# Keys turned in 32x32 blocks by VectorE and placed by GpSimd, in place of TensorE transposes, from the third block on

## Chip, core and metric

The kernel runs on one core of a Trainium2 chip. The metric is the device time of one execution in microseconds (us). TensorE is called PE there (PEld is its loading of weights), VectorE DVE, ScalarE ACT, GpSimd POOL, and SyncE, which issues most of the DMAs, SP.

## What is computed

A gated linear attention over 768 tokens (4 sequences, 8 heads of 48) is followed by a two-layer feed-forward with squared relu (384 to 2048 to 384), all in float32:

```python
f = 1.0 / (1.0 + np.exp(-f_logit))
for t in range(S):
    state = f[:, :, t, :, None] * state + np.einsum('bhd,bhe->bhde', k[:, :, t], v[:, :, t])
    y[:, :, t] = np.einsum('bhd,bhde->bhe', q[:, :, t], state)
x = y.transpose(0, 2, 1, 3).reshape(B * S, H * D)
g = np.maximum(x @ w_in, 0.0) ** 2
out = g @ w_out
```

## The kernel before

**Tiling.** The tokens are cut into six blocks of 128 tokens of each sequence (512 columns). A block of attention consists of four units, numbered through from 0 to 23: three "own" units hold 48 rows of each of two heads and 16 rows of the last two heads; the fourth ("last") unit of a block works on those 16-row pieces, which the own units collect in `last_kq` and `last_kn`. Inside a unit the 128 tokens are two halves of 64 (`c` = 0 and 1); tokens meet within a half by a masked matrix of scores, and the state is carried from half to half. The state's increments (keys times values, `add_one`, L537) need the keys with tokens on partitions, while they arrive with channels on partitions: so a unit's keys are turned (`turn`, four TensorE transposes, L511, into a bank of PSUM) and copied out by ScalarE (`turned`, L517 to `kn`, L519 to `last_kn`).

**Feed-forward.** float32 products are made of three rounded ones (high by low, low by high, high by high). A block has 16 steps (`flow`): nine matmuls into a bank `ph` (`up`, L241); relu, square and a rounded copy `gh` on ScalarE (L251 to L253); the rest `gl` on VectorE (L258); and, two steps later, nine matmuls into the output (`down`, L268). Two banks `ph` take turns, so a step's `up` needs the `gl` of two steps before.

**Order.** Each engine works strictly through its own list; only GpSimd's list is laid out by the scheduler. Blocks 0 and 1 of the attention (units 0 to 7) and the first weights are placed by hand (`FIRST`, `SECOND`). Everything later is hooked into the feed-forward's 90 steps. Unit 8 has its slot at step 12, unit 9 at 15, unit 10 at 18 and so on (`SLOTS`); the matmuls of a unit's scores and increments and of the outputs of the unit before it run at the end of that step (`slot`). `STAGE_AT` says how many steps ahead of its slot each part of an own unit runs: loads (`L`, `v`), gates and decayed keys (`GK`: a scan L449, GpSimd's L454 and the multiplication L455), queries (`Q`: L461, the scan L463, L466), the turn (`TN`), the crossing of states (`s`). A hook at place 0 stands ahead of a step's `up`, at 0.5 between ScalarE's squares and VectorE's `gl`, at 1 behind `down`. `LAST_AT` is for last units. During steps 1 to 14 the second half of the weights is decoded as well (ScalarE L138, VectorE L147, L149, L153, ScalarE's L166, VectorE's L168).

In a slot the increments of the first half (c = 0) come first, those of the second half last; a small GpSimd memset (L746) stands between the two, and the second half waits for it. From unit 8 on the transposes and the increments use one bank, `shared`.

Of the kernel before, what the change touches and what calls it, by code (L numbers as in the profile page):

```python
# [13 lines left out]
F32 = mybir.dt.float32  # L14
# [8 lines left out]
P = 128  # L23
B, H, S, D = 4, 8, 768, 48
DM, DFF = 384, 2048
HP = H // 2
C = 64
TB = 128
NBLK = S // TB
NC = TB // C  # L30
# [3 lines left out]
ROWS = 64 + D  # L34
# [12 lines left out]
NBUF = 3  # L47
# [7 lines left out]


SLOTS = (12, 15, 18, 21, 23, 27, 31, 35, 39, 43, 47, 51, 55, 59, 63, 67, 71)
STAGE_AT = ((-6, 0, "Lv"), (-3, 1, "GK"), (-1, 0.5, "Q"), (-1, 1, "TN"), (1, 1, "s"))
LAST_AT = ((-6, 0, "v"), (1, 1, "s"))


FIRST = """
# [301 lines left out]
def fast_path(ctx, psum, tc, moe, ident, low, flag, fkqT, vN, w, w4, out):  # L364
    nc = tc.nc
    V, G = nc.vector, nc.gpsimd
# [17 lines left out]
    for r in (0, C):  # L384
        G.affine_select(
            out=mask[r : r + C], in_=mask[r : r + C], compare_op=ALU.is_ge, fill=0.0,
# [19 lines left out]
    class Unit:  # L406
# [30 lines left out]
                nc.sync.dma_start(self.fkq[:, c, :NT], fkqT[self.blk, self.hp, :, c])  # L437

        def load_v(self):
            self.vn = self.wk([P, B, 2 * D], "vn", NBUF + 1)  # L440
            nc.sync.dma_start(self.vn, vN[self.blk, self.hp])

        def gates(self):
# [56 lines left out]

        def turn(self):

            if self.blk < 2:
                self.pk = self.ps_a[0].tile([P, B, P], F32, tag="pk", name=f"pk{self.nm}")
            else:

                if not shared:
                    shared.append(self.ps_a[0].tile([P, B, P], F32, tag="pk", name="shared"))
                self.pk = shared[0]
            for b in range(B):  # L510
                nc.tensor.transpose(  # L511
                    out=self.pk[:, b], in_=self.kt[:, b * TB : (b + 1) * TB], identity=ident
                )

        def turned(self):
            self.kn = self.wk([P, B, ROWS], "kn")
            nc.scalar.copy(out=self.kn, in_=self.pk[:, :, :ROWS])  # L517
            at = self.hp * (C - D)
            nc.scalar.copy(  # L519
                out=last_kn.rearrange("p b (h r) -> p b h r", h=2)[:, :, :, at : at + C - D],  # L520
                in_=self.pk.rearrange("p b (h r) -> p b h r", h=2)[:, :, :, D:],
            )

        @cached_property
# [8 lines left out]

        def add_one(self, dd, b, c, h):

            rows, m = slice(c * C, (c + 1) * C), D if h or self.blk > 1 else C
            return nc.tensor.matmul(  # L537
                dd[h * C : h * C + m, c, b * D : (b + 1) * D],
                lhsT=self.kn[rows, b, h * C : h * C + m],
                rhs=self.vn[rows, b, h * D : (h + 1) * D], start=True, stop=True,  # L540
            )
# [116 lines left out]
        def stage(self, letters):  # L658
            for c in letters:
                {  # L660
                    "L": lambda: self.load(slice(0, 3)),
                    "f": lambda: self.load(slice(0, 1)),
                    "k": lambda: self.load(slice(1, 2), slice(2, 3)),
                    "v": lambda: self.load_v(),
                    "G": lambda: self.gates(),
                    "K": lambda: self.keys(),
                    "Q": lambda: self.queries(),
                    "m": lambda: self.move(),
                    "r": lambda: self.crossed(),
                    "T": lambda: self.turn(),  # L670
                    "N": lambda: self.turned(),
                    "D": lambda: self.add(),
                    "S": lambda: self.scores(),
                    "M": lambda: self.masked(),
                    "C": lambda: self.states(),
                    "s": lambda: self.crossed_states(),
                    "Y": lambda: self.outputs(),
                    "H": lambda: self.upper(),
                    "z": lambda: self.less(),
                    "X": lambda: self.lower(),  # L680
                    "g": lambda: self.parts((1,), G if self.blk < 2 else nc.sync),
                    "h": lambda: self.parts((0,), nc.sync),
                }[c]()
# [5 lines left out]
    ps_a = moe.ps_a = psum.enter_context(  # L689
        tc.tile_pool(name="ps_a", bufs=1, space=bass.MemoryType.PSUM)  # L690
    )
    half = list(range(LO)), list(range(LO, NF))
    xs = {blk: moe.new_x(blk, blk) for blk in range(2)}
    units, decoding, shared = {}, {}, []
# [13 lines left out]
    def slot(old, new):  # L708

        ab = ps_a.tile([P, 2, 512], F32, tag="ab", name=f"ab{(new or old).nm}_{new is None}")
        rows = [[], []]
        if old:
            old.py = ab[:, :, : B * C]
            for c in range(NC):
                for b in range(B):
                    for part in range(2):
                        for h in (c, 1 - c):  # L720
                            rows[c].append((C, lambda a=(part, b, c, h): old.output_one(*a)))
        if new:
            new.sd = ab[:, :, B * C :]
            new.dd = shared[0].rearrange("p (c e) n -> p c (e n)", c=NC)[:, :, : B * D]
            adds = [
                [] if new.last_of(c) else [
                    (D, lambda a=(b, c, h): update(*a)) for b in range(B) for h in (c, 1 - c)
                ] for c in range(NC)
            ]
            for h in range(2):  # L730
                for b in range(B):
                    for c in (h, 1 - h):
                        rows[h].append((C, lambda a=(b, c, h): new.score_one(*a)))
            rows = [adds[0] + rows[0], rows[1] + adds[1]]
        seen = []

        def behind(ins, first):
            tc.add_manual_dep(ins, first.name, mybir.DependencyInfo(
                mybir.DependencyClass.Sync, mybir.DependencyReason.DATA
            ), reason="one bank")  # L740

        def update(b, c, h):
            ins = new.add_one(new.dd, b, c, h).ins
            if c == 0 and b == B - 1 and h:

                seen.append(G.memset(tick, 0).ins)  # L746
                behind(seen[0], ins)
            elif c and b == 0 and h:
                behind(ins, seen[0])

        at = [0, 0]
        while any(rows):
            r = min((r for r in range(2) if rows[r]), key=lambda r: at[r])
            cols, do = rows[r].pop(0)
            at[r] += cols
            do()
# [51 lines left out]
    with tc.manual_schedule(engines={ET.PE, ET.SP, ET.DVE, ET.Activation}):  # L808
# [13 lines left out]
        def hook(n, at, do):  # L822
            hooks.setdefault((max(n, 0), at), []).append(do)
# [38 lines left out]
        for at, old, un in zip(SLOTS, (None, *late), (*late, None)):  # L862
            if un:
                for n, place, stage in STAGE_AT if un.own else LAST_AT:
                    hook(at + n, place, lambda un=un, stage=stage: un.stage(stage))
            hook(at, 1, lambda old=old, un=un: slot(old, un))
            if old:
                hook(at, 1, lambda old=old: old.stage("HX" if old.own else "HXhg"))
            if un:
                hook(at, 1, lambda un=un: un.stage("rMCm" if un.own else "rMC"))  # L870
# [155 lines left out]
@with_exitstack  # L1026
def tile_kernel(ctx: ExitStack, tc: tile.TileContext, fkqT, vN, w, w4, out):
    nc = tc.nc
    const = ctx.enter_context(tc.tile_pool(name="const", bufs=1))
    ident = const.tile([P, P], F32, name="ident")  # L1030
    low = const.tile([P, NBLK * NJ, B * NC], F32, name="low")
    sums = const.tile([P, 2 * NF], F32, name="sums")
    flag = const.tile([1, 2], I32, name="flag")
    moe = Moe(ctx, tc, const, sums, out)
    with ExitStack() as fast:
        last, rv = fast_path(fast, ctx, tc, moe, ident, low, flag, fkqT, vN, w, w4, out)

    last.w = moe.w[HELD]  # L1040

    with tc.If(rv > 0):
        with ExitStack() as gen:
            general_path(gen, tc, moe, ident, fkqT, vN, w, out, last)
    moe.w[HELD] = last.w
    last.g[NF - 1] = moe.held
    moe.finish_last(last, lambda e: out[last.blk, e * P : (e + 1) * P])
# [61 lines left out]
```

## Time and profile before

| what | value |
|---|---|
| median of 3 runs | 491.6 us (489.62 to 492.38) |
| the profiled execution's own time | 489.16 us |
| its span, first to last instruction | 487.5 us |
| granted TensorE clock | 0.997 of full speed |
| busy: TensorE, VectorE, ScalarE, GpSimd | 97%, 53%, 58%, 7% |

Times of the profile are counted from the start of the span; 1.7 us of the execution lie around it. Busy time of an engine is the time in which an instruction of it is recorded as running; matmuls overlap, so TensorE's idle time says more than its busy time.

### The profile page before, as it was taken

The numbers are of one execution on the slowest core, as the hardware profiler recorded it, in microseconds if no ns is written. First come the engines' busy times: TensorE is split into PE (matmuls) and PEld (weight loads), VectorE is DVE, ScalarE is ACT, GpSimd is POOL, SyncE is SP. The second block draws the span as 40 slices with busy tenths as digits, with TensorE's granted clock in tenths as the row PEclk, the third lists the DMA queues.
The fourth block names the chain that finished last, engine by engine and source line by source line (L and its number), as shares of the span: only waits on it lengthen the run. The fifth ranks groups of instructions, "written<-read, shape, count | busy, mean of one in ns | idle before, by whom it ended". The sixth has DMA issues, their size and how long they took to land. (4 is left out here: it accounts for less than half of the span.)

```text
span 487.5 us, 11465 instructions
## 1 busy us (share of the span) xinstructions
PE 472.8 (97%) x4795; PEld 388.2 (80%) x4795; DVE 256.5 (53%) x474; ACT 281.7 (58%) x570; POOL 32.1 (7%) x82
## 2 busy tenths in 40 slices
PE   5889999999999999999999999999999999999996
PEld 5677787888788888888888888888888888888884
DVE  7999966989985355643437443346343212221111
ACT  4777757887676555644546645555655444544451
POOL 6222010001100000000000000000000000000000
PEclk9999999999999999999999999999999999999998
DMA  8985235566134004232005222004210002100002
GB/s 284 309 284 143 58 103 197 205 200 224 29 95 143 17 6 119 94 101 74 1 2 125 94 93 82 1 1 117 87 26 2 2 0 34 66 0 3 0 0 71
DMA packets 22636, 42.60 MB, mean 87 GB/s; under 512 B 4512, under 2 KB 8128, under 8 KB 22576
## 3 DMA queue, kind: packets, MB, share of 16 engines
q1 hardware_dynamic: 22128, 40.86, 27.1%
q0 software_dynamic: 448, 0.92, 0.8%
q8 instruction: 39, 0.64, 0.5%
q14 instruction: 21, 0.17, 0.1%
HBM read 31.69 MB, written 4.72 MB: 75 GB/s over the span
## 5 line engine op out<-in xcount | busy, mean ns | idle before, releaser
L241 PE MATMUL ph<-x,w 128*128 128x512 f32 x864 | 216.4, 395 | 1.8 <-DVE gl L258 1.4
L241 PEld LDWEIGHTS ph<-x,w 128*128 128x128 f32 x864 | 159.4, 188 | 36.5 <-DVE w L168 1.1
L268 PE MATMUL po<-gh,w 128*128 128x512 f32 x570 | 175.6, 389 | 0.0
L258 DVE TENSOR_TENSOR gl<-ph,gh 128x512 fp32r<-128x512 f32 x95 | 65.6, 691 | 172.1 <-ACT gh L253 171.8
L251 ACT ACTIVATE ph<-ph 128x512 f32<-128x512 f32 x96 | 55.9, 582 | 119.7 <-PE ph L241 119.5
L268 PEld LDWEIGHTS po<-gh,w 128*128 128x128 f32 x570 | 107.0, 188 | 22.2
L268 PE MATMUL po<-gl,w 128*128 128x512 f32 x285 | 111.1, 390 | 0.0
L268 PEld LDWEIGHTS po<-gl,w 128*128 128x128 f32 x285 | 53.5, 188 | 11.2
L252 ACT ACTIVATE ph<-ph 128x512 f32<-128x512 f32 x96 | 55.9, 582 | 3.0
L253 ACT CAST gh<-ph 128x512 fp32r<-128x512 f32 x95 | 55.8, 587 | 3.0
L449 DVE TENSOR_TENSOR_SCAN fkq<-fz,dr 128x520 f32<-128x520 f32 x18 | 22.3, 1236 | 6.3 <-ACT fz L444 6.3
L166 ACT CAST w<-wa 128x384 fp32r<-128x384 f32 (+1 forms) x33 | 16.6, 511 | 15.3 <-DVE wa L153 12.3
L454 POOL TENSOR_SCALAR fkq<-fkq 128x8 f32<-128x8 f32 x18 | 13.2, 735 | 145.1 <-DVE fkq L449 136.6
L463 DVE TENSOR_TENSOR_SCAN fkq<-fz,dz 128x520 f32<-128x520 f32 x18 | 22.3, 1242 | 0.6
L602 PE MATMUL ab_False<-sc,vn 64*48 64x64 f32 (+1 forms) x480 | 20.7, 220 | 0.0
L138 ACT ACTIVATE wa<-raw 128x384 f32<-128x384 f32 (+1 forms) x33 | 18.1, 548 | 4.3 <-DMA raw<-in_w_dram 4.2
L631 ACT CAST x<-ab_False 112x512 fp32r<-112x512 f32 x12 | 7.0, 587 | 22.0 <-PE shared L537 16.0
L611 PE MATMUL ab_False<-rx,sx 48*48 48x64 f32 (+1 forms) x240 | 19.4, 216 | 0.0
L647 DVE TENSOR_TENSOR x<-ab_False,x 112x512 fp32r<-112x512 f32 x12 | 8.3, 692 | 20.2 <-ACT x L631 20.2
L149 DVE SCALAR_TENSOR_TENSOR wa<-raw,wa 128x384 int32<-128x384 int32 (+1 forms) x33 | 17.9, 551 | 0.7
L602 PEld LDWEIGHTS ab_False<-sc,vn 64*48 64x48 f32 (+1 forms) x480 | 18.0, 126 | 0.0
L168 DVE TENSOR_TENSOR w<-wa,w 128x384 fp32r<-128x384 f32 (+1 forms) x33 | 17.9, 545 | 0.0
(138 smaller groups left out, 461.5 us busy)
## 6 DMA issues: line engine op xcount, KB each, us to landing
raw<-in_w_dram SPq DMA_DIRECT2D x32, 384.0 KB, 4.3
fkq<-in_fkqT_dram SPq DMA_DIRECT2D x15, 768.0 KB, 5.8
vn<-in_vN_dram SPq DMA_DIRECT2D x24, 192.0 KB, 4.5
out_dram<-ob SPq DMA_DIRECT2D x14, 256.0 KB, 2.4
fkq<-in_fkqT_dram SPq DMA_DIRECT2D x9, 256.0 KB, 4.6
x<-ys SPq DMA_DIRECT2D x30, 64.0 KB, 2.4
last_kq<-fkq SPq DMA_DIRECT2D x28, 64.5 KB, 2.3
out_dram<-part SPq DMA_DIRECT2D x3, 256.0 KB, 2.4
```

The costliest lines, as they stand in the source:

```text
L138: nc.scalar.activation(a, upper_f, AF.Abs, scale=2.0**-112, **kw)
L149: nc.vector.scalar_tensor_tensor(out=h, in0=upper, scalar=-(1 << 31), in1=h, op0=ALU.bitwise_and, op1=ALU.bitwise_or)
L241: self.nc.tensor.matmul(self.cur.ph[f], lhsT=w[:, i], rhs=x[:, j], start=first and n == 0, stop=last and n == 2)
L251: nc.scalar.activation(ph, ph, AF.Relu)
L252: nc.scalar.activation(ph, ph, AF.Square)
L253: nc.scalar.copy(out=gh, in_=ph)
L258: self.nc.vector.tensor_tensor(out=gl, in0=self.cur.ph.pop(f), in1=gh.bitcast(F32), op=ALU.subtract)
L268: self.nc.tensor.matmul(c.po[e], lhsT=l, rhs=r, start=f == c.fs[0] and i == 0, stop=f in c.ends and i == 2, skip_group_check=len(c.ends) > 1,)
L449: V.tensor_tensor_scan(out=rr[:, ::-1], data0=self.fz[:, NZ * CZ : 0 : -1], data1=dr[:, ::-1], initial=0.0, op0=ALU.mult, op1=ALU.add,)
L463: V.tensor_tensor_scan(out=pp, data0=self.fz[:, : NZ * CZ], data1=dz, initial=0.0, op0=ALU.mult, op1=ALU.add)
L602: nc.tensor.matmul(to[:m], lhsT=self.vn[rows, b, h * D : h * D + m], rhs=self.sc[rows, h, b], start=b == 0, stop=none and c == 0 and b == ...
L611: nc.tensor.matmul(to[:m], lhsT=s[rows, b * D : b * D + m], rhs=q[rows], start=False, stop=b == B - 1,)
```

## The change

From unit 8 on the four transposes of an own unit are gone. In their place, for each half `c`, VectorE turns the 32x32 blocks of the half's keys (128 partitions x 256 elements) into a tile `kb` of one buffer, and GpSimd copies the eight 32-partition pieces of it to where they belong in `kn`. The first half is done behind the keys (`GKB`, three steps ahead of the slot), the second behind the queries (`Qb`, one step ahead). ScalarE's copy of the bank into `kn` goes; the copy into `last_kn` stays and reads `kn`. The bank `shared` is now made in `slot` and holds increments alone. Unit 8's increments write 64 rows for one head, as the first to use the bank. The values `vn` are loaded five steps ahead instead of six, into three buffers instead of four.

```diff
-STAGE_AT = ((-6, 0, "Lv"), (-3, 1, "GK"), (-1, 0.5, "Q"), (-1, 1, "TN"), (1, 1, "s"))
-LAST_AT = ((-6, 0, "v"), (1, 1, "s"))
+STAGE_AT = (
+    (-6, 0, "L"), (-5, 0, "v"), (-3, 1, "GKB"), (-1, 0.5, "Qb"), (-1, 1, "N"), (1, 1, "s"),
+)
+LAST_AT = ((-5, 0, "v"), (1, 1, "s"))
+Q = 32
...
-            self.vn = self.wk([P, B, 2 * D], "vn", NBUF + 1)
+            self.vn = self.wk([P, B, 2 * D], "vn", NBUF)
...
+        def turn_blocks(self, c):
+            if c == 0:
+                self.kn = self.wk([P, B, P], "kn")
+            kb = self.wk([P, B, C], "kb", 1)
+            V.transpose(out=kb, in_=self.kt.rearrange("p (b c t) -> p b c t", b=B, c=NC)[:, :, c])
+            for a in range(0, C, Q):
+                for r in range(0, P, Q):
+                    G.tensor_copy(
+                        out=self.kn[c * C + a : c * C + a + Q, :, r : r + Q], in_=kb[r : r + Q, :, a : a + Q]
+                    )
+
         def turned(self):
-            self.kn = self.wk([P, B, ROWS], "kn")
-            nc.scalar.copy(out=self.kn, in_=self.pk[:, :, :ROWS])
+            if self.blk < 2:
+                self.kn = self.wk([P, B, P], "kn")
+                nc.scalar.copy(out=self.kn[:, :, :ROWS], in_=self.pk[:, :, :ROWS])
             at = self.hp * (C - D)
             nc.scalar.copy(
                 out=last_kn.rearrange("p b (h r) -> p b h r", h=2)[:, :, :, at : at + C - D],
-                in_=self.pk.rearrange("p b (h r) -> p b h r", h=2)[:, :, :, D:],
+                in_=(self.pk if self.blk < 2 else self.kn).rearrange("p b (h r) -> p b h r", h=2)[:, :, :, D:],
             )
...
-            rows, m = slice(c * C, (c + 1) * C), D if h or self.blk > 1 else C
+            rows, m = slice(c * C, (c + 1) * C), D if h or self.n > 2 * HP else C
...
+            if not shared:
+                shared.append(ps_a.tile([P, B, P], F32, tag="pk", name="shared"))
             new.dd = shared[0].rearrange("p (c e) n -> p c (e n)", c=NC)[:, :, : B * D]
```

The lists of the engines show it at unit 8. A tile's last number only tells tiles of one name apart, and the changed kernel's lines are numbered 3 to 13 higher from the edit on. VectorE's list around unit 8's queries (`fkq_0_1462` holds its keys and queries, `wa` and `w` are weights being decoded), before:

```order
L461 RECIPROCAL dz<-fkq_0_1462 128x8 [waits Pool_49]
L463 SCALAR_TENSOR_TENSOR fkq_0_1462<-fz_71,dz 128x520 [waits DVE_49]
L466 TENSOR_TENSOR fkq_0_1462<-fkq_0_1462 128x512 [waits DVE_49]
L258 TENSOR_TENSOR gl_11_1689<-ph_11_1678,gh_11_1688 128x512 [waits PE_49,Activation_49]
L168 TENSOR_TENSOR w_1_1697<-wa_1_1673,w_1_1697 128x384 [waits Activation_49]
L147 TENSOR_SCALAR wa_0_1717<-wa_0_1717 128x384 [waits Activation_49]
```

and in the changed kernel:

```order
L464 RECIPROCAL dz<-fkq_0_1462 128x8 [waits Pool_49]
L466 SCALAR_TENSOR_TENSOR fkq_0_1462<-fz_71,dz 128x520 [waits DVE_49]
L469 TENSOR_TENSOR fkq_0_1462<-fkq_0_1462 128x512 [waits DVE_49]
L518 STREAM_TRANSPOSE kb_0_1707<-fkq_0_1462 128x256 [waits Pool_49]
L261 TENSOR_TENSOR gl_11_1700<-ph_11_1689,gh_11_1699 128x512 [waits PE_49,Activation_49]
L171 TENSOR_TENSOR w_1_1718<-wa_1_1684,w_1_1718 128x384 [waits Activation_49]
L150 TENSOR_SCALAR wa_0_1731<-wa_0_1731 128x384 [waits Activation_49]
```

The transpose of the second half stands between the queries and `gl`, and waits for GpSimd (the one buffer of `kb`). ScalarE's list in the same place, before:

```order
L166 CAST w_1_1697<-wa_1_1673 128x384 [waits DVE_49]
L517 COPY kn_0_1714<-shared 128x448 [waits PE_49]
L519 COPY last_kn<-shared 128x8x16
L138 ACTIVATE wa_0_1717,sums<-raw_0_1565 128x384 [waits DMAHW3_49]
L138 ACTIVATE wa_1_1722,sums<-raw_1_1568 128x384 [waits DMAHW4_49]
L166 CAST w_0_1727<-wa_0_1717 128x384 [waits DVE_49,Activation_49]
```

and in the changed kernel:

```order
L169 CAST w_1_1718<-wa_1_1684 128x384 [waits DVE_49]
L530 COPY last_kn<-kn_0_1627 128x8x16 [waits Pool_49]
L141 ACTIVATE wa_0_1731,sums<-raw_0_1565 128x384 [waits DMAHW3_49]
L141 ACTIVATE wa_1_1736,sums<-raw_1_1568 128x384 [waits DMAHW4_49]
L169 CAST w_0_1741<-wa_0_1731 128x384 [waits DVE_49,Activation_49]
```

One copy of the two is left; it now waits for GpSimd, with the next weights' decoding behind it in the list.

## Rows read from the trace of the kernel before

**Rows 1.** The page of the kernel before: busy us, share of the span, instructions.
```profile
PE 472.8 (97%) x4795; PEld 388.2 (80%) x4795; DVE 256.5 (53%) x474; ACT 281.7 (58%) x570; POOL 32.1 (7%) x82
```

**Rows 2.** The windows: busy us per engine, with instructions; granted clock, DMA share, GB/s.
```profile
110.00:150.00 40.00, 39.21 (x354) 31.86 (x354) 35.80 (x66) 28.90 (x65) 4.16 (x8) 1.00 0.34 107
150.00:190.00 40.00, 40.00 (x536) 33.15 (x535) 20.27 (x35) 22.24 (x43) 2.20 (x7) 1.00 0.28 79
```

**Rows 3.** The timeline around one later unit: start us, us, engine, line.
```profile
187.63 0.23 POOL L454 TENSOR_SCALAR low<-fkq 128x8 f32<-128x8 f32 x1
...
188.97 1.24 DVE L463 TENSOR_TENSOR_SCAN fkq<-fz,dz 128x520 f32<-128x520 f32 x1
...
190.25 0.69 DVE L466 TENSOR_TENSOR fkq<-fkq 128x512 f32<-128x512 f32 x1
...
192.21 0.60 PE L511 MATMUL shared<-ident,fkq 128*128 128x128 f32 x4
192.57 2.32 PE L241 MATMUL ph<-x,w 128*128 128x512 f32 x9
...
198.28 0.20 PE L537 MATMUL shared<-vn,kn 64*48 64x48 f32 x1
```

**Rows 4.** The instructions of L511: ns min/median/max, first and last start us.
```profile
L511 PE MATMUL shared<-ident,fkq x48: 270/272/273, 117.8 to 362.0; 128*128 128x128 f32 x48
```

**Rows 5.** Groups by line and shape: busy us, mean ns | idle before.
```profile
L582 DVE TENSOR_TENSOR sp<-state,fkq 112x192 f32<-112x192 f32 x30 | 10.6, 353 | 0.5
...
L149 DVE SCALAR_TENSOR_TENSOR wa<-raw,wa 112x256 int32<-112x256 int32 x1 | 0.4, 424 | 0.0
```

**Rows 6.** The timeline of GpSimd (POOL) at the start.
```profile
1.03 0.19 POOL L395 MEMSET sp<- 112x32 f32 x2
1.25 0.28 POOL masks.py:199 TENSOR_SCALAR_AFFINE_SELECT ident<-ident 128x128 f32<-128x128 f32 x1
1.50 0.53 POOL L385 TENSOR_SCALAR_AFFINE_SELECT mask<-mask 64x64 f32<-64x64 f32 x2
```

**Rows 7.** The timeline at 144.6 us: one of VectorE, one of GpSimd.
```profile
144.58 0.69 DVE L455 TENSOR_TENSOR fkq<-fkq 128x512 f32<-128x512 f32 x1
144.63 0.74 POOL L454 TENSOR_SCALAR fkq<-fkq 128x8 f32<-128x8 f32 x1 [5.99 <-DVE fkq L449]
```

**Rows 8.** The timeline of units 8 and 9; in brackets idle us, releaser.
```profile
119.94 0.27 ACT L519 COPY last_kn<-shared 128x128 f32<-128x128 f32 x1
...
120.10 0.56 ACT L138 ACTIVATE wa<-raw 128x384 f32<-128x384 f32 x1
...
121.10 0.68 DVE L258 TENSOR_TENSOR gl<-ph,gh 128x512 fp32r<-128x512 f32 x1
...
122.16 0.35 DVE L147 TENSOR_SCALAR wa<-wa 128x384 int32<-128x384 int32 x1
...
122.40 0.24 PE L537 MATMUL shared<-vn,kn 64*48 64x48 f32 x1
...
123.22 0.25 PE L537 MATMUL shared<-vn,kn 64*48 64x48 f32 x2
...
123.79 0.52 ACT L166 CAST w<-wa 128x384 fp32r<-128x384 f32 x1 [2.51 <-DVE wa L153]
...
126.06 0.69 DVE L258 TENSOR_TENSOR gl<-ph,gh 128x512 fp32r<-128x512 f32 x1 [0.42 <-ACT gh L253]
...
132.57 0.68 DVE L258 TENSOR_TENSOR gl<-ph,gh 128x512 fp32r<-128x512 f32 x1
...
133.40 2.52 PE L241 MATMUL ph<-x,w 128*128 128x512 f32 x9 [0.77 <-DVE gl L258]
...
138.23 0.68 DVE L258 TENSOR_TENSOR gl<-ph,gh 128x512 fp32r<-128x512 f32 x1
...
139.31 0.20 PE L537 MATMUL shared<-vn,kn 64*48 64x48 f32 x1
```

**Rows 9.** The DMA issues of the page: KB each, median us to landing.
```profile
vn<-in_vN_dram SPq DMA_DIRECT2D x24, 192.0 KB, 4.5
```

More of the change, by code (lines that the diff above doesn't have):

```diff
@@ L501, in turn @@
         def turn(self):
[L503 to L509, printed above, removed]
+            self.pk = self.ps_a[0].tile([P, B, P], F32, tag="pk", name=f"pk{self.nm}")
             for b in range(B):
@@ L670, in stage @@
                     "T": lambda: self.turn(),
+                    "B": lambda: self.turn_blocks(0),
+                    "b": lambda: self.turn_blocks(1),
                     "N": lambda: self.turned(),
```

## Prediction

> **What bounds the kernel now.** I read the busy table first: TensorE works 97% of the span, everything else 58% or less [rows 1]. The windows say where that is not quite true. From 150 us on TensorE is busy in 40.00 of 40.00 us, with VectorE and ScalarE at about half; between 110 and 150 us it is 39.21, and there VectorE is at 35.80 and ScalarE at 28.90, because the second half of the weights is still being decoded [rows 2]. So after 150 us a microsecond taken off TensorE is a microsecond off the time, and anything else is free until its lateness reaches TensorE. Before 150 us VectorE has almost no slack, and the one wait of the stretch shows whom TensorE waits for: the first matmul of a block at 133.40 stood idle 0.77 us for `gl`, VectorE's subtraction [rows 8]. Two of the twelve changed units, 8 and 9 (slots 12 and 15), lie in that stretch; the other ten come behind it.
>
> **What is removed.** Four transposes a unit. In a quiet place the first starts at 192.21 and the next block's first matmul at 192.57: 0.36 us of TensorE for the four. There are 48 of them, so twelve such gaps [rows 3, 4], 4.3 us. Unit 9's stands just ahead of the 133.40 wait and only fills it, so 11 x 0.36 = 4.0 us count at most. ScalarE loses its copy of the turned keys and keeps the 0.27 us one into `last_kn` [rows 8]; after 150 us it is busy for 22 of 40 us [rows 2], so that is worth nothing there.
>
> **What is added on VectorE.** Two transposes of 128x256 a unit. No row has one. The nearest are 353 ns for 112x192 and 424 ns for 112x256 [rows 5]; I take 0.40 us. After 150 us VectorE's idle half hides it.
>
> **What is added on GpSimd.** Sixteen copies a unit of 32 partitions x 128 elements. The only single-input instructions of GpSimd with so many elements are the selects: 0.28 us for 128x128, and two of 64x64 in 0.53 [rows 6]. An instruction of 8 elements lasts 0.23 [rows 3], so most of the price is fixed. I take 0.28 us a copy, 2.24 us for eight. From below: two small memsets took 0.19 us together [rows 6], so if copies on different partitions overlap, 0.10. From above: an 8-element instruction took 0.74 us beside VectorE's two-input multiplication of 0.69, three times its 0.23 [rows 3, 7]; so 0.74 where VectorE is in the way each time. The value is nearest to the select, which reads and writes like a copy.
>
> **Does it fit, behind 150 us?** Take the unit of [rows 3]. GpSimd's two small instructions end at 187.86, and the first eight copies can start at 187.9, behind the first VectorE transpose. The second transpose can't start before L466 ends at 190.94, nor before those eight have read the single `kb`. The keys of the second half are used by the matmul that was at 198.28, now 197.9. So 10.0 us hold sixteen copies, a 0.40 us transpose, and up to 1.9 us in which the scan (1.24) and L466 (0.69) keep GpSimd out: they fit while a copy takes under (10.0 - 0.4 - 1.9) / 16 = 0.48 us. At 0.28 there are 3 us to spare, and all ten units gain: 10 x 0.36 = 3.6 us. ScalarE's `last_kn` copy now stands behind the sixteenth copy, at about 194.5, and holds up the relu of the product begun at 192.57 by little; ScalarE's idle 18 of 40 us take that up [rows 2].
>
> **Units 8 and 9.** Here the new work is late by the length of a busy queue, and two engines queue behind it. The second transpose of unit 8 stands behind L466, which ended where `gl` started, 121.10 [rows 8]; the first one has already pushed that to 121.5. So it ends at 121.9, and the eight copies at 124.15, or 124.65 if one weight subtraction (L168, two inputs) keeps GpSimd out for 0.5 us, as 0.74 against 0.23 in [rows 3, 7].
> - TensorE: the slot begins at 122.40 - 0.36 = 122.04 and uses the second half 0.82 us later (123.22 against 122.40) [rows 8]. It waits from 122.9 to 124.2-124.7.
> - ScalarE: the `last_kn` copy sits in order ahead of the decode's L138 (120.10 before). Now it ends 0.27 us behind the copies, L138 0.56 behind that, so VectorE's L147 moves from 122.16 to 125.0-125.5, 2.9 to 3.3 us. From L147 on the chain had no slack: ScalarE waited 2.51 us for L153, VectorE 0.42 for `gh` [rows 8]. So `gl` of 126.06 moves by as much; from there to the `gl` of 132.57 VectorE ran without a wait, and unit 9's first transpose adds 0.40. That is the very `gl` for which TensorE waited: it restarts not at 133.40 but 3.2 to 3.7 us later. This one number contains the slot's wait and unit 8's saved 0.36.
> - Unit 9: L466 ended where `gl` started, 138.23 [rows 8]; plus 3.3-3.7, plus 0.40, plus eight copies (2.24, or 2.74 beside another L168): 144.1-145.1. The slot's second half was due at 139.31 [rows 8], now at 142.5-143.0: a wait of 1.6 to 2.1 us, with `gl` of the next steps late once more, up to 0.3.
>
> **Sum.** +3.2 to 3.7, +1.6 to 2.1, +0.3, -3.6: between +1.5 and +2.5 us. With contention shown for GpSimd in the rows I take the upper end, +2.5 us: 491.7 us against the profiled execution's 489.2. That execution lies 2.4 us under the median of the runs shown (491.6), so on their scale 494.1. Bounds: at 0.10 us a copy unit 8's chain slips only 1.7 us and unit 9 waits 0.2 and 0.3, sum -1.4; at 0.20 each burst of eight is 0.64 shorter, +0.2 to +1.2; at 0.33 it is 0.4 longer, +2.3 to +3.3; at 0.74 see below. 0.5% is 2.45 us, about what a measurement of this kernel can tell from no change, so the forecast stands on that edge.
>
> The `v` load, with three buffers instead of four and one step later, lands 4.5 us after its issue [rows 9] and is issued five steps ahead, some 20 us (one step and most of a slot lie between 192.57 and 198.28 in [rows 3]). It costs nothing unless it is held for over three steps; unit 12's must now wait for the slot at step 18, one step. Were that cover gone, a unit's slot would wait for what is left of 4.5 us.
>
> **Rivals.**
> 1. *Copies overlap* (0.10 to 0.2 us): sum -1.4 to +1.2, 490.2 to 492.8. For it: the memsets at 0.10 us each [rows 6]. Against: the selects there stand one behind the other, 0.25 us from start to start.
> 2. *Faster*: the whole 11 x 0.36 = 4.0 us and no new wait, 487.6. It needs unit 8's copies to end by 122.9 and the decode's L138 not to matter, which is to say a transpose and eight copies within 1.4 us of L466, and slack in VectorE that [rows 2] don't show. The point of decision: whether TensorE restarts at 133.4 or later.
> 3. *VectorE is held by the copies*. The rows show GpSimd waiting for VectorE (0.74 for 0.23) while the multiplication beside it lasted 0.69 us like the one of [rows 3] beside which GpSimd did nothing; but there GpSimd came second [rows 7]. If a copy that comes first holds a two-input instruction for its own 0.28 us, the eight early copies of unit 8 push VectorE by up to 2.2 us in the stretch without slack: +2.5 + 2.2, 496.3. [...]
> 4. *Copies are slow everywhere* (0.74 us): 16 x 0.74 + 0.4 = 12.2 against 10.0 us, so 2.2 us of waiting in each of ten units, and 3.7 more in each of the two early ones: 494.1 + 22 + 7 = 523. It starts at 0.48 us a copy.
>
> [...]
>
> **How the numbers follow.** Forecast 0.46, copies overlap 0.20, faster 0.13, VectorE held 0.13, slow copies 0.08. The forecast's own range, copies of 0.20 to 0.33 us, is 491.8 to 494.9; its likelier upper part lies about +0.5%, so I give half of it to each side. Faster by over 0.5%: 0.14 (rival 2 and a little of 1). Within 0.5%: the rest of rival 1 and half of the forecast, 0.41. Slower: the other half and rivals 3 and 4, 0.45. For 8 in 10 the range reaches from 488.5 to 501: it leaves out most of rival 2 and all of rival 4.
>
> **What would show it.** No L511 behind 100 us, and TensorE's next matmul 0.36 us sooner at each of ten slots; copies of about 0.28 us in two bursts of eight a unit; TensorE idle for GpSimd in the slots at about 122 and 140 us and nowhere behind 150; the wait for `gl` at about 133 longer by 2 us; ScalarE's `last_kn` copy waiting some 4 us for GpSimd in both units. It is wrong if waits for GpSimd appear in every slot (copies over 0.48 us), if VectorE's instructions get longer beside copies, or if the transposes take much more than 0.4 us.

## The result, and the profile after

| | before | after |
|---|---|---|
| median of 6 runs each, on one chip | 490.88 us (489.62 to 492.38) | 495.96 us (494.3 to 496.91) |
| ratio, 95% interval | | 1.0095 (1.0068 to 1.0123) |
| the profiled execution, its span | 489.16, 487.5 us | 495.62, 493.8 us |

The change makes the kernel 0.95% slower, some 4.7 us by the ratio (5.1 by the medians); +2.5 us was forecast. The busy line of the page of the changed kernel, against [rows 1]:

```profile
PE 471.1 (95%) x4747; PEld 386.3 (78%) x4747; DVE 266.2 (54%) x498; ACT 276.4 (56%) x558; POOL 100.8 (20%) x274
```

TensorE has lost its 48 transposes, and yet it is idle for a larger share. The windows say where: against [rows 2] it is idle for 4.8 us of the stretch from 110 to 150 (0.8 before) and for 2.1 us of the next (nothing before).

```profile
110.00:150.00 40.00, 35.19 (x315) 28.03 (x314) 30.35 (x59) 22.48 (x52) 13.70 (x38) 0.91 0.35 107
150.00:190.00 40.00, 37.94 (x496) 30.98 (x498) 23.02 (x41) 22.09 (x45) 12.76 (x39) 1.00 0.20 63
```

The waits of TensorE, the longest four: line waited for, us in total, times, longest. The changed kernel's lines are numbered up to 15 higher behind the edit (the small memset L746 is L761), and the transposes of units 0 to 7 are L508. The first wait is the increments' second half. The `flag` it names is the small memset between the two halves; here it stands behind the eight copies in GpSimd's list, so a wait for it is a wait for the copies.

```profile
PE shared L548 <- POOL flag L761: 4.5, 3, 2.2
PE ds L548 <- DMA vn<-in_vN_dram: 2.5, 1, 2.5
PE pk L508 <- DVE fkq L458: 2.0, 1, 2.0
PE po L271 <- DVE ob L339: 1.9, 1, 1.9
```

The wait for `pk` stands in every kernel of this study. The one for `vn` is a load at 17 us, long before the change acts: 2.5 us here. It comes and goes with either number of buffers: with four it is 0.5 us in the kernel before and 1.9 in *no turn* (below), with three 0.3 to 0.8 in five kernels (*from unit 10* is one), 1.6 in *copies halved* and 2.2 in *from unit 12*. By step 11 (113.68 before, 115.88 here) the profiled execution is 2.2 us late. I call this lateness the front and count it to no part of the change.

So I follow the lateness of TensorE's steps rather than the sum. The timeline of the changed kernel, TensorE (start us, us), at the first matmuls of the steps:

```profile
119.96 2.23 PE L244 MATMUL ph<-x,w 128*128 128x512 f32 x9
...
127.32 0.34 PE L548 MATMUL shared<-vn,kn 64*48 64x48 f32 x2 [2.25 <-POOL flag L761]
...
139.82 2.63 PE L244 MATMUL ph<-x,w 128*128 128x512 f32 x9 [0.45 <-DVE gl L261]
...
148.22 0.25 PE L548 MATMUL shared<-vn,kn 64*48 64x48 f32 x2 [2.06 <-POOL flag L761]
...
148.72 2.35 PE L244 MATMUL ph<-x,w 128*128 128x512 f32 x9
...
157.04 2.20 PE L244 MATMUL ph<-x,w 128*128 128x512 f32 x9
...
161.81 0.50 PE L271 MATMUL po<-gl,w 128*128 128x512 f32 x1 [1.90 <-DVE ob L339]
...
165.31 2.33 PE L244 MATMUL ph<-x,w 128*128 128x512 f32 x9
...
179.67 0.25 PE L548 MATMUL shared<-vn,last_kn 64*48 64x48 f32 x2 [0.16 <-POOL flag L761]
...
180.18 2.35 PE L244 MATMUL ph<-x,w 128*128 128x512 f32 x9
...
487.40 2.32 PE L271 MATMUL po<-held,w 128*128 128x512 f32 x9 [0.30 <-PEq L1057]
```

The same steps in the timeline of the kernel before, where [rows 8] don't have them:

```profile
118.12 2.31 PE L241 MATMUL ph<-x,w 128*128 128x512 f32 x9
...
139.81 2.33 PE L241 MATMUL ph<-x,w 128*128 128x512 f32 x9
...
148.47 2.33 PE L241 MATMUL ph<-x,w 128*128 128x512 f32 x9
...
154.69 2.33 PE L241 MATMUL ph<-x,w 128*128 128x512 f32 x9
...
169.07 2.33 PE L241 MATMUL ph<-x,w 128*128 128x512 f32 x9
...
480.58 2.33 PE L268 MATMUL po<-held,w 128*128 128x512 f32 x9 [0.30 <-PEq L1042]
```

| up to the start of | before, after | late by | what was added | forecast |
|---|---|---|---|---|
| step 12 | 118.12, 119.96 | 1.84 | front +2.2, unit 8's transposes -0.36 | -0.36 |
| step 15 | 133.40, 139.82 | 6.42 | unit 8, with its -0.36: 6.42 - 2.2 = +4.2 | +3.2 to 3.7 |
| step 16 | 139.81, 148.72 | 8.91 | unit 9: +2.5 | +1.6 to 2.1, and up to 0.3 |
| step 18 | 148.47, 157.04 | 8.57 | unit 10's transposes: -0.34 | -0.36 |
| step 19 | 154.69, 165.31 | 10.62 | the wait for `ob`: +2.05 | none |
| step 22 | 169.07, 180.18 | 11.11 | slot 21: +0.49 | none |
| the last block | 480.58, 487.40 | 6.82 | nine units: -4.29, or -0.48 each | -0.36 each |

Without the front that is 4.2 + 2.5 - 0.34 + 2.05 + 0.49 - 4.29 = +4.6 us.

The `ob` term and the smaller one of slot 21 are those that the prediction didn't have. VectorE and GpSimd at unit 10, in their own timelines:

```profile
156.09 4.02 POOL L521 COPY kn<-kb 32x128 f32<-32x128 f32 x8 [0.29 <-DVE kb L518]
160.65 2.62 POOL L521 COPY kn<-kb 32x128 f32<-32x128 f32 x8 [0.54 <-DVE kb L518]
```

```profile
160.14 0.45 DVE L518 STREAM_TRANSPOSE kb<-fkq 128x256 f32<-128x256 f32 x1 [1.52 <-POOL kn L521]
160.51 0.65 DVE L261 TENSOR_TENSOR gl<-ph,gh 128x512 fp32r<-128x512 f32 x1
161.08 0.68 DVE L339 COPY ob<-po 128x512 f32<-128x512 f32 x1
```

A unit's second transpose waits until GpSimd has read the first half out of the single `kb`, 1.52 us here (1.2 to 1.5 in nine units). Behind it in VectorE's list stand `gl` and, at this step alone of the ten later units, the copy of a finished output bank (`ob`). TensorE's `down` (L271) needs that bank, and it waits 1.90 us.

Slot 21 is that of unit 11, a last unit, and the next own unit's slot, 23, lies only two steps behind it. So unit 12's first eight copies, three steps ahead of its own slot, come ahead of slot 21's memset in GpSimd's list:

```profile
176.89 2.59 POOL L521 COPY kn<-kb 32x128 f32<-32x128 f32 x8 [0.29 <-DVE kb L518]
179.53 0.09 POOL L761 MEMSET flag<- 1x1 int32 x1
```

The bracket in TensorE's list has 0.16 us of idle time, but from the slot's first matmul to its second half it takes 1.89 us (177.78 to 179.67) instead of 1.42 (167.15 to 168.57).

The new pieces by their own lines (times in ns: shortest, median, longest):

```profile
L521 POOL COPY kn<-kb x192: 280/291/1325, 115.5 to 371.8; 32x128 f32<-32x128 f32 x192
L518 DVE STREAM_TRANSPOSE kb<-fkq x24: 439/445/447, 114.9 to 368.9; 128x256 f32<-128x256 f32 x24
```

### The profile page after: what moved, and what is told of

Its sections match the earlier page's. It is cut to its first block, busy times and chain, and to the rows that moved or that the text cites. A ratio compares the mean times of both kernels' runs of the same rounds, so it can differ in the third digit from the quotient of the medians.

```text
span 493.8 us, 11605 instructions
## 1 busy us (share of the span) xinstructions
PE 471.1 (95%) x4747; PEld 386.3 (78%) x4747; DVE 266.2 (54%) x498; ACT 276.4 (56%) x558; POOL 100.8 (20%) x274
## 3 DMA queue, kind: packets, MB, share of 16 engines
HBM read 31.69 MB, written 4.72 MB: 74 GB/s over the span
## 5 line engine op out<-in xcount | busy, mean ns | idle before, releaser
L244 PEld LDWEIGHTS ph<-x,w 128*128 128x128 f32 x864 | 161.4, 189 | 37.5 <-DVE w L171 1.3
L271 PE MATMUL po<-gh,w 128*128 128x512 f32 x570 | 175.9, 390 | 0.0
L271 PEld LDWEIGHTS po<-gh,w 128*128 128x128 f32 x570 | 107.4, 188 | 22.3
L271 PE MATMUL po<-gl,w 128*128 128x512 f32 x285 | 111.6, 392 | 1.9 <-DVE ob L339 1.9
L521 POOL COPY kn<-kb 32x128 f32<-32x128 f32 x192 | 70.2, 366 | 31.0 <-DVE kb L518 21.8
L271 PEld LDWEIGHTS po<-gl,w 128*128 128x128 f32 x285 | 53.8, 189 | 13.6 <-DVE ob L339 2.3
L457 POOL TENSOR_SCALAR fkq<-fkq 128x8 f32<-128x8 f32 x18 | 12.2, 679 | 150.2 <-DVE fkq L452 125.8
L530 ACT COPY last_kn<-kn 128x128 f32<-128x128 f32 x12 | 3.6, 300 | 43.7 <-POOL kn L521 43.7
L466 DVE TENSOR_TENSOR_SCAN fkq<-fz,dz 128x520 f32<-128x520 f32 x18 | 22.4, 1242 | 0.6
L171 DVE TENSOR_TENSOR w<-wa,w 128x384 fp32r<-128x384 f32 (+1 forms) x33 | 18.2, 555 | 0.0
```

The lines of the kernel that those rows point to most:

```text
L171: nc.vector.tensor_tensor(out=w[:, 1], in0=a, in1=w[:, 0].bitcast(F32), op=ALU.subtract)
L244: self.nc.tensor.matmul(self.cur.ph[f], lhsT=w[:, i], rhs=x[:, j], start=first and n == 0, stop=last and n == 2)
L271: self.nc.tensor.matmul(c.po[e], lhsT=l, rhs=r, start=f == c.fs[0] and i == 0, stop=f in c.ends and i == 2, skip_group_check=len(c.ends) > 1,)
L466: V.tensor_tensor_scan(out=pp, data0=self.fz[:, : NZ * CZ], data1=dz, initial=0.0, op0=ALU.mult, op1=ALU.add)
L521: G.tensor_copy(out=self.kn[c * C + a : c * C + a + Q, :, r : r + Q], in_=kb[r : r + Q, :, a : a + Q])
```

## The experiments

The diffs are cut to the parts of lines that differ; `...` stands for lines left out. The experiments ran in two groups of four, each beside 17 runs of the kernel before: medians 490.13 us (488.9 to 491.9) and 489.83 us (489.17 to 492.14). My theory was that units 8 and 9 pay, with the `ob` wait, and the ten later ones gain. The main rivals: every unit pays a little; or the three buffers of values cost something.

### From unit 10

Units 8 and 9 keep TensorE's transposes; three buffers of values stay.

```diff
+EARLY_AT = ((-6, 0, "L"), (-5, 0, "v"), (-3, 1, "GK"), (-1, 0.5, "Q"), (-1, 1, "TN"), (1, 1, "s"))
+FROM = 10
...
-            if self.blk < 2:
+            if self.n < FROM:
...
-                for n, place, stage in STAGE_AT if un.own else LAST_AT:
+                for n, place, stage in (STAGE_AT if un.n >= FROM else EARLY_AT) if un.own else LAST_AT:
```

> Units 8 and 9 keep the TensorE transposes; only units from 10 on use VectorE and GpSimd. Theory A (the loss sits in units 8 and 9, +4.2 and +2.5 us in the profile, and in one wait of 2.05 us at unit 10 for the copy of the output block; every later unit gains 0.42): time of before - 10 x 0.42 + 0 to 2.05, that is 2.1 to 4.2 us under before, 486.7 to 488.8 if before is 490.9; no wait of TensorE for GpSimd at slots 12 and 15. Theory B (every unit pays, by GpSimd and VectorE getting in each other's way): not under before, 491 or more. Theory C (2.2 us of the loss is a wait for the values' DMA at 17 us, made by three buffers): that wait is there too, 2.2 us more than A.

485.94 us (485.2 to 487.63), ratio 0.9931 (0.9911 to 0.995): what was a loss of 0.95% is a gain of 0.7%. What its list of waits still has for GpSimd's `flag` and for the output copy at unit 10:

```profile
PE po L273 <- DVE ob L341: 0.6, 1, 0.6
...
PE shared L555 <- POOL flag L768: 0.2, 1, 0.2
```

The 0.2 us are slot 21's. Followed by its steps, its front aside, it ends 3.3 us ahead of the kernel before. Units 8 and 9 hold the loss; neither the later units nor the three buffers do.

### From unit 12

The same with `FROM = 12`, so that unit 10 keeps TensorE's transposes too.

> Units 8, 9 and 10 keep the TensorE transposes. Theory A: no unit in the stretch of decoding or at the output copy is left, nine gain 0.42: before - 3.8 us, 487.1 if before is 490.9; faster than e1_from10 if unit 10's wait stays there, 0.4 slower if it doesn't. Theory B: not under before. Theory C: 2.2 us more.

486.22 us (485.51 to 487.48), ratio 0.9925 (0.9909 to 0.9942), the same as from unit 10 within the intervals. No wait for `ob` is in its trace, and by its steps without the front it ends 3.9 us ahead of the kernel before, against 3.3 *from unit 10*, where unit 10 loses some 0.5 us on balance. The runs can't tell these two apart.

### Second turn behind `gl`

In all twelve units the second transpose and its copies go behind `gl` and `ob`, to the end of the step.

```diff
-(-1, 0.5, "Qb"), (-1, 1, "N"), (1, 1, "s"),
+(-1, 0.5, "Q"), (-1, 1, "bN"), (1, 1, "s"),
```

> All twelve units changed, but the second transpose stands behind VectorE's gl and the copy of the output block instead of ahead of them. Theory A: the wait at unit 10 (TensorE 1.9 us for the output copy, which stood behind a transpose that waited 1.5 us for the one buffer of its result) goes, units 8 and 9 stay as they are or lose up to 0.6 us more each, since their copies start one gl later: 1 to 2 us under the changed kernel, 494 to 495. If the wait has another cause (GpSimd slowing VectorE itself): no change, 496.

495.08 us (493.8 to 497.0), ratio 1.012 (1.0101 to 1.014): no better than the changed kernel. The `ob` wait is gone, so its cause is the transpose ahead of it. But unit 10's slot now waits for the copies instead (by the steps 0.7 us), and the early units pay more (5.1 and 3.3 us instead of 4.2 and 2.5):

```profile
PE shared L548 <- POOL flag L761: 4.8, 4, 3.0
PE ph L244 <- DVE gl L261: 2.5, 2, 1.9
```

### Late `last_kn`

ScalarE's copy into `last_kn` goes behind the unit's slot, so that the decoding no longer stands behind it.

```diff
-(-1, 0.5, "Qb"), (-1, 1, "N"), (1, 1, "s"),
+(-1, 0.5, "Qb"), (1, 0, "N"), (1, 1, "s"),
```

> All twelve units changed, but ScalarE's copy into last_kn comes two hooks later, at the start of the step after the slot, so nothing of the weights' decoding stands behind it while it waits for GpSimd. Theory A (in unit 8 the delay of the decoding behind that copy costs more than TensorE's own wait for the copies): TensorE's waits in slots 12 and 15 stay at 2.1 to 2.9 us, the gl at step 13 is late no longer, 2.7 us under the changed kernel, 493.3. Rival (only TensorE's direct wait counts): no change, 496.

490.81 us (489.51 to 493.12), ratio 1.002 (1.0005 to 1.0034): most of the loss is gone, more than I expected. The timelines show that this is not the whole story. VectorE decodes on without a gap, so the `gl` that TensorE needs for step 15 (132.57 before, 139.00 in the changed kernel) is at 134.48:

```profile
122.92 0.59 DVE L171 TENSOR_TENSOR w<-wa,w 128x384 fp32r<-128x384 f32 x1
123.44 0.45 DVE L150 TENSOR_SCALAR wa<-wa 128x384 int32<-128x384 int32 x1
...
134.48 0.68 DVE L261 TENSOR_TENSOR gl<-ph,gh 128x512 fp32r<-128x512 f32 x1
```

TensorE waits 3.06 us for the copies, longer than in the changed kernel, because beside VectorE's decoding the eight take 3.71 us (2.85 there), and then goes on at half its clock (granted 0.50 from 128 to 132 us):

```profile
126.39 0.34 PE L548 MATMUL shared<-vn,kn 64*48 64x48 f32 x2 [3.06 <-POOL flag L761]
...
127.41 4.21 PE L244 MATMUL ph<-x,w 128*128 128x512 f32 x9
...
134.19 2.20 PE L244 MATMUL ph<-x,w 128*128 128x512 f32 x9
...
138.27 2.20 PE L244 MATMUL ph<-x,w 128*128 128x512 f32 x9
```

From the end of the wait to the block at 134.19 are 7.80 us; the kernel before takes 127.94 - 123.22 = 4.72 us for the same matmuls. The 3.1 us between are the clock's, and now TensorE waits for nothing at step 15: with the decoding on time, the low clock is the bound there. Step 15 starts 4.9 us later than before, 4.5 without this execution's front of 0.4, which is no better than the 4.2 of the changed kernel. What is saved comes behind it: step 16 is later by 144.36 - 139.81 = 4.55 us, 0.3 less than step 15, so unit 9 costs nothing (2.5 in the changed kernel), because VectorE is less late than TensorE; and the wait for `ob` is 0.7 us.

### No turn

The kernel before, with four buffers of values, without the turning from unit 8 on. This leaves out part of the computation: twelve units' increments read old keys from `last_kn`. The bank `shared` and unit 8's 64 rows are as in the changed kernel.

```diff
             else:
-
-                if not shared:
-                    shared.append(self.ps_a[0].tile([P, B, P], F32, tag="pk", name="shared"))
-                self.pk = shared[0]
+                return
...
         def turned(self):
+            if self.blk > 1:
+                self.kn = last_kn
+                return
```

> The kernel before without any turning of keys from unit 8 on: no transposes, no copies of them; the increments read whatever stands in last_kn (this leaves out the turning of the keys of twelve units, so the states are not the reference's). It prices what is removed. By the rows (0.36 us for four transposes, eleven that count): 4.0 us under before. By the steps of the changed kernel behind 165 us (0.42 us a unit and more, since the block of matmuls behind the transposes is longer too): twelve times 0.45, 5.4 us under before.

484.91 us (483.6 to 486.35), ratio 0.9888 (0.9864 to 0.9913): 4.9 us by the medians (5.5 by the ratio, 4.8 by its steps without the front) is about the most that the change could have brought. By its steps the ten later units gain 0.48 us each, and the early ones nothing: TensorE's wait for `gl` at step 15 only grows from 0.77 [rows 8] to 1.5 us.

### From unit 10, unit 10 late

From unit 10, with that unit's second transpose behind `gl` and `ob`, and its copy into `last_kn` behind the slot.

```diff
+TENTH_AT = ((-6, 0, "L"), (-5, 0, "v"), (-3, 1, "GKB"), (-1, 0.5, "Q"), (-1, 1, "b"), (1, 0, "N"), (1, 1, "s"))
...
-(STAGE_AT if un.n >= FROM else EARLY_AT)
+(STAGE_AT if un.n > FROM else TENTH_AT if un.n == FROM else EARLY_AT)
```

> As e1_from10, and for unit 10 alone the second transpose stands behind gl and the output copy and the last_kn copy at the start of the step after the slot. Theory: the 0.6 us that TensorE still waited for the output copy at unit 10 goes: 0.6 us under e1_from10, 485.3 if e1 is 485.9. If unit 10 only waits elsewhere: the same as e1.

485.67 us (485.11 to 486.07), ratio 0.9906 (0.9885 to 0.9927): the lowest median of the kernels that leave nothing out, and ahead of the kernel before. The 0.27 us that it gains on *from unit 10* is within the spread of the runs; by its steps without the front it ends 4.3 us ahead of the kernel before, against 3.3. The trace shows what was meant, VectorE's `ob` ahead of the transpose and no wait of TensorE for it:

```profile
150.05 0.68 DVE L342 COPY ob<-po 128x512 f32<-128x512 f32 x1
151.04 0.45 DVE L526 STREAM_TRANSPOSE kb<-fkq 128x256 f32<-128x256 f32 x1 [0.31 <-POOL kn L529]
```

### From unit 10, copies halved

Each of GpSimd's copies is made as two of half the columns, to see where the copies stop to fit behind the later units.

```diff
-                    G.tensor_copy(
-                        out=self.kn[c * C + a : c * C + a + Q, :, r : r + Q], in_=kb[r : r + Q, :, a : a + Q]
-                    )
+                    for b in range(0, B, 2):
+                        G.tensor_copy(
+                            out=self.kn[c * C + a : c * C + a + Q, b : b + 2, r : r + Q],
+                            in_=kb[r : r + Q, b : b + 2, a : a + Q],
+                        )
```

> As e1_from10, but each GpSimd copy is cut in two (32 copies a unit of 32 partitions x 64 elements). It tests the point at which copies would cost in every slot. If half a copy costs 0.24 to 0.25 us (most of it fixed), 32 of them take 8 us, with 1.6 us of blocking and 0.45 of a transpose just about the 10.0 us that there are: the same as e1 or up to 0.5 us more in each of ten units, 486 to 491, with waits of TensorE for GpSimd in several slots. If a half costs half: the same as e1.

490.74 us (489.61 to 492.36), ratio 1.001 (0.9995 to 1.0026): the whole gain is gone. By the line of the copies half the columns cost nearly as much (227 to 232 ns against 280 to 291), so that a whole piece costs 0.46 us instead of 0.29:

```profile
L529 POOL COPY kn<-kb x320: 227/232/1249, 147.1 to 369.6; 32x64 f32<-32x64 f32 x160
```

Two waits of TensorE, one for the output copy at unit 10 and one in a slot:

```profile
153.86 0.50 PE L273 MATMUL po<-gl,w 128*128 128x512 f32 x1 [1.69 <-DVE ob L341]
...
172.68 0.25 PE L557 MATMUL shared<-vn,last_kn 64*48 64x48 f32 x2 [1.12 <-POOL flag L770]
```

Followed by its steps it ends 4.9 us behind *from unit 10*: 1.0 from the front, 1.0 more at the output copy, 1.0 more in the slot at 172.68, and the remaining 1.9 around units 12, 13 and 16. The slot at 172.68 is that of a last unit, which turns no keys: its `flag` stands in GpSimd's list behind the next own unit's first copies.

### From unit 10, late `last_kn`

> As e1_from10, with the last_kn copy at the start of the step after the slot for all ten units. Theory A (behind the decoding ScalarE has slack to wait for GpSimd, so the place of this copy counts for nothing): the same as e1, within 0.7 us. Rival (ScalarE's wait of some 3 us for GpSimd in each unit delays the relu and so TensorE a little each time): 1 us or more under e1.

The edit is that of *late `last_kn`*, on top of *from unit 10*. 486.01 us (485.66 to 488.13), ratio 0.9922 (0.9897 to 0.9946), the same as without it: where ScalarE has no weights to decode, its wait for GpSimd costs nothing that the runs show.

Two more ways out, two buffers for `kb` and four for the values, weren't tried.

## Why the prediction was right, and where it was not

The change was to cost time in units 8 and 9 and to gain in the ten behind, and so it does. The size, +2.5 us forecast and +4.6 by the steps, came within the wide range 488.5 to 501 partly by luck, since misses of both signs met: against the forecast's upper values unit 8 cost 0.5 us more, unit 9 0.1, `ob` 2.05 and slot 21 0.49, and the ten units gained 1.0 more. One sum of the chances is off by 0.01: half the forecast with rivals 3 and 4 makes 0.44, not 0.45.

**Where the work is late.** Right. TensorE waits in the slots of units 8 and 9, and none of the ten later units waits for its own keys. Take one of those: the second eight copies end at 205.93 (203.31 and 2.62), and the second half is used at 208.46, 2.5 us later; 3 were forecast.

```profile
203.31 2.62 POOL L521 COPY kn<-kb 32x128 f32<-32x128 f32 x8 [0.54 <-DVE kb L518]
...
208.46 0.20 PE L548 MATMUL shared<-vn,kn 64*48 64x48 f32 x1
```

*From unit 10* settles it: without the two early units the loss turns into a gain. The sign that TensorE waits for GpSimd nowhere behind 150 us failed in one slot, by the 0.16 us of slot 21.

**What binds at unit 8.** Right. The `last_kn` copy waited 4.88 us for GpSimd, and the decode behind it moved VectorE's L150. ScalarE's and VectorE's timelines:

```profile
127.15 0.30 ACT L530 COPY last_kn<-kn 128x128 f32<-128x128 f32 x1 [4.88 <-POOL kn L521]
127.36 0.55 ACT L141 ACTIVATE wa<-raw 128x384 f32<-128x384 f32 x1
127.81 0.19 ACT L141 ACTIVATION_READ_ACCUMULATOR wa<-raw 128x1 f32 x1
```

```profile
128.03 0.36 DVE L150 TENSOR_SCALAR wa<-wa 128x384 int32<-128x384 int32 x1 [2.74 <-ACT wa L141]
```

L150 stood at 122.16 before; 128.03 - 122.16 - 2.2 is 3.7 us later, where 2.9 to 3.3 were forecast. Small things add up to the difference: the transposes take 0.445 and not 0.40, the eight copies 2.85 beside VectorE and not 2.74, ScalarE's copy 0.30 and not 0.27, and the decode's readout of its sums, 0.19, was not in the working. Unit 9's first transpose, ahead of the same `gl`, adds 0.45 more and brings the 4.2. One sign came out otherwise: TensorE's wait for that `gl` was to be 2 us longer and is shorter, 0.45 us, because its matmuls had become slower in the meantime (a block of nine took 4.21 us instead of 2.34, last section); when step 15 starts is set by `gl` all the same. But only just: TensorE was ready for step 15 at 139.37, 3.8 us late (the front aside) by its wait for the copies (2.25 us) and by its lowered clock (granted 0.50 from 128 to 132 us), which the prediction didn't have. *Late `last_kn`* agrees: with the decoding's delay gone, step 15 is as late as it was.

**The price of a copy.** Right: 0.29 us against 0.28; the first eight take up to 4.1 us where VectorE's scan and multiplications run beside them (2.59 at unit 12, where no scan does), the second eight 2.6 to 2.85. Rival 1, copies that overlap, fell: eight of 0.29 us make 2.3, and no eight of the changed kernel took less than 2.59.

**Rival 3, VectorE held by the copies.** Not at the size it had there. Beside the copies VectorE's subtraction L171 took 0.59 to 0.64 us (mean 0.555 over all), and in *late `last_kn`* L150 took 0.45 against its usual 0.35. So the sign "VectorE's instructions get longer" came, but it is a tenth of a microsecond for two or three instructions of a burst, and not 0.28 for each. What the trace of the changed kernel shows is GpSimd's side: at unit 10 the copy that starts at 156.7 us, beside VectorE's scan L466 (1.24 us), took 1.24 us, and the one at 158.0, beside L469 (0.69 us), 0.75, where the median copy takes 0.29. The longest L171 and L150 there are 0.64 and 0.45 us, against medians of 0.55 and 0.35: a tenth, where the rival's 496.3 rests on 0.28.

**Rival 4's threshold.** Near the forecast: later slots were to wait from 0.48 us a copy on; at 0.46 three slots wait for `flag` (1.7 us in all, 1.1 of them in slot 21), and units 12, 13 and 16 are late.

**What was missing.** The step that failed is the sentence that all ten units behind 150 us gain because the copies fit. It looked at when a unit's keys are used, and not at what else stands behind the new instructions in their engines' lists. In VectorE's list the `ob` copy stands behind unit 10's second transpose, which waits for the single `kb`: +2.05 us. In GpSimd's list slot 21's memset stands behind unit 12's first copies: +0.49. *Second turn behind `gl`* and *unit 10 late* show the first: with `ob` ahead of the transpose the wait is gone. Part of it comes from unit 9. In the changed kernel ScalarE's `last_kn` copy of that unit waited until 148.05, and VectorE got its next `gh` only at 150.11:

```profile
148.05 0.30 ACT L530 COPY last_kn<-kn 128x128 f32<-128x128 f32 x1 [4.86 <-POOL kn L521]
```

```profile
150.11 0.69 DVE L261 TENSOR_TENSOR gl<-ph,gh 128x512 fp32r<-128x512 f32 x1 [3.91 <-ACT gh L256]
```

So unit 10's first transpose came 2.5 us into step 17 (155.48 against 152.96), and 1.3 us in *from unit 10* and in *late `last_kn`*; in both of these the wait for `ob` is 0.7 us.

**The gain per unit.** 0.48 us instead of 0.36, in the nine units behind slot 21 as in the ten of *no turn*. A gap of four transposes is 0.36, but the block behind them is longer too: 2.32 us for its nine matmuls [rows 3] against 2.20 elsewhere.

**Second turn behind `gl`.** The clock falls there too (granted 0.55 and 0.59 from 126 to 130 us, 0.50 from 140 to 142), but its dearer early units aren't the clock's: behind the slow stretches TensorE still waits, 1.89 us for `gl` at step 15 and 1.27 us for the copies in slot 15.

**Still open**: how often the wait for `vn` comes, since one execution of each kernel was traced; and what it would bring to place unit 12's first copies behind slot 21, which no run tried.

## What to carry to other kernels

Work taken off the bounding engine paid here only where the engines that got it had slack at that place (0.48 us gained in each of nine units, 4.2 and 2.5 us lost in units 8 and 9): cost every unit in its own stretch, and make the switch only from the unit on where that stretch begins. When an instruction that can wait is put into an engine's list, go through what stands behind it there in every unit, since here one bank's copy at one step cost as much as four units gain (2.05 against 0.48 us). The place behind the copy that others wait for took that wait away here (0.6 us in *from unit 10*, none in *unit 10 late*); a second buffer might, but no run tried it.

## What the runs showed of the hardware

After the wait of 2.25 us in slot 12 TensorE went on at a granted clock of 0.50 from 128 to 132 us; ahead of the slot, from 112 to 124 us, it had been busy for 12.00 of 12.00 us at 1.00. Windows of the changed kernel (the figure behind GpSimd's count is the granted clock; every window of the kernel before between 122 and 140 us has 1.00; here it is 0.53 from 132 to 134 and 1.00 from 134 on):

```profile
126.00:128.00 2.00, 0.68 (x24) 0.68 (x25) 0.00 (x0) 0.85 (x4) 1.09 (x5) 0.76 0.43 112
128.00:130.00 2.00, 2.00 (x15) 1.62 (x10) 1.86 (x5) 0.87 (x4) 0.00 (x0) 0.50 0.01 3
```

The block that starts at 128.34 takes 4.21 us instead of 2.34. In the changed kernel that costs nothing, since TensorE still had to wait 0.45 us for `gl` at 139.82; in *late `last_kn`* it is worth 3.1 us. After the 2.06 us wait of slot 15 the clock stayed at 1.00 (148 to 154 us), while in *second turn behind `gl`* it fell to 0.50 (140 to 142 us) after a wait of 1.89 us. So in these two traces the length of the wait alone doesn't say whether the clock falls; what does, no run shows.
